# Two kinds of loads put behind small VectorE memsets, a longer pause ahead of the taps, and new shares for the convolution in a fused H3 and feed-forward kernel

## The chip, the cores and the metric

The kernel runs on one core of one Trainium2 chip. The metric is the device time of one execution in microseconds (us). The number given for a kernel is the median of several executions; the profile is of one execution, taken by the hardware profiler.

## The reference

For x of 2048 rows by 576 columns, the result is x plus two branches that both read the layer-normalised x. One is a feed forward with 4608 hidden columns; the other is an H3 block, a short convolution over four rows, a product with v, a convolution as long as the sequence, and a gate by the normalised x. In outline, with the shapes in comments:

```python
xn = _layernorm(x)                          # 2048 x 576
# feed forward
h = maximum(xn @ w1, 0)                     # 576 x 4608
ffn = h @ w2                                # 4608 x 576
# H3
k_shift = sum(k[rows - 3 + j] * shift_k[:, j] for j in range(4))
kv = k_shift * v
y = irfft(rfft(kv, 4096) * rfft(ssm_k, 4096))[:2048] + kv * ssm_D
return x + xn * y + ffn
```

## The kernel before

**Two strands on one TensorE.** The feed forward is the main strand. The 2048 rows are 16 tiles of 128 rows, in four blocks of four tiles (512 rows). Its hidden columns are 18 pairs of 256 columns, and `n` counts pairs: `n` = 0 to 17 for blocks 0 and 1, then `n` = 18 to 35 for blocks 2 and 3 (the second half; the change between them is the half turn). All products run in a 12 bit split: every operand is a rounded part and a rest, and three products of parts make one. In the first half the hidden values come from `mm1` (L513, psh), in the second from `quad` (L489, psa and psb), which needs seven block products in place of eight. `relu` makes the rounded hidden part hh on ScalarE (L495) and the rest ll on VectorE (L496). `unit` (L576, pso) multiplies with w2, and VectorE adds the result to the accumulator tiles acc (L580 and L584).

**Weights.** `load_w1(n)` brings one pair's first weights into the raw tile r1, of which there is one buffer: a 512 KB load (L395) and two small ones (L397). `load_w2` (L404) brings 288 KB into r2, two buffers. ScalarE rounds them (g at L413, w at L475), POOL (GpSimd) makes the rests (L384). In this text g1_0 is the first g made of pair 1's r, which the order prints as g_0 out of r_1, and r_1 that raw tile. A raw tile can be loaded again once POOL has read it for the last time.

**Normalised rows.** Blocks 0 and 1 are normalised and transposed at the start (`first_xT`, `second_xT`): statistics (L171, L172), `inv_std` (L178 to L183, with one square root on ScalarE, L179), the normalisation (L186) and the transposes on TensorE (L252 and L268). Blocks 2 and 3 are prepared during the first half by `later_xT`, piece by piece: it loads a block's rows into a scratch tile (L303, rows), takes their statistics, normalises, transposes, splits and stores the results to HBM as kept_b1, kept_b2, kept_t and kept_xr. `fetch` brings them back around the half turn.

**The convolution** is the other strand, a generator, `conv`. It has four stages. FK turns the filter: 12 loads of 384 KB bring it into the tile kr (L650), VectorE transposes pieces of it (L664, tr), `stack` splits them (L619 on ScalarE, L620 on VectorE, ks), and TensorE multiplies (L626). FX does the same with the input: the four taps (L725, L728, L729), the product with v (`gate`, L734), `stack` (xs), TensorE (L626, psf out of xs and wx), and the result zx goes to HBM. FM (L807) multiplies in the frequency domain, and FO (L958, L959) turns back what FM stored as zy; its loads are zo (L894), its splits ohi and olo (L914, L915).

**What sets the order.** After every few matmuls of the feed forward, `tick` is called with their cost in columns. It adds cost times a rate to the convolution's budget, and when the budget allows runs the next step of `conv`. A step yields a positive weight (W_FK, W_FX, W_FM, W_FO), which is taken from the budget, or a negative number, a pause: no step until so much of the feed forward has passed. START is the pause ahead of the first step. A step with `with here():` may be issued only behind the last accumulate and the last relu that the program has given out so far; a step without it has no such tie, and a scheduler lays it on its engine as early as its inputs and buffers let it. Nearly all loads go through one queue, SP, in the order in which they are issued, and each of SP's transfers waits for the one eight before it (its semaphore is one of DMAHW0 to DMAHW7).

**What the change touches.** The rows' loads in `later_xT` (L302 to L304), the filter's loads in `conv` (L646 to L652), the constants at L50, L55, L58 and L59, and the steps ahead of the loop over `T` in FX (L742 to L754).

Of the kernel before, what the change touches and what calls it, by code (L numbers as in the profile page):

```python
# [19 lines left out]
D = 576  # L20
# [3 lines left out]
NH = D // 2  # L24
# [7 lines left out]
BT = T // NB  # L32
# [14 lines left out]
W_STAGE = (12 * HR, 12 * HR, 12 * HR + 2 * 512, 6 * HR + 2 * 512)  # L47
W_UNIT = 12 * NH
PAUSE = 16000
START = 4000  # L50
SHARE = 0.96


N_FK, N_FX, N_FM, N_FO = 4 * T, 4 * T, 6 * NG, 4 * T
W_FK, W_FX, W_FM, W_FO = 1.75, 4.3, 1.62, 2.65  # L55
Q = 32
KB = 3
KT_GAP = 4500  # L58
PAUSES = 4 * NH // Q // KB * KT_GAP / PAUSE + 8  # L59
FFT_TOTAL = N_FK * W_FK + N_FX * W_FX + N_FM * W_FM + N_FO * W_FO  # L60
W_QUAD = sum(W_STAGE)
FFN_TOTAL = NPAIR * HB * (W_PLAIN + W_QUAD + 2 * 4 * W_UNIT)
# [47 lines left out]
def h3_ffn_kernel(ctx: ExitStack, tc, x, k, v, shift_k, ssm_k, ssm_D, w1, w2, fwd, inv, mid, out):  # L110
    nc = tc.nc
    x = x[0].rearrange("(p u t) d -> u p t d", u=U, t=T)
# [35 lines left out]
    def halves(u):  # L148

        return slice(u * A1, (u + 1) * A1), slice((1 - u) * A1, (2 - u) * A1)  # L150

    def move(tile_, rows, t, store=False, queues=(nc.sync, nc.sync)):
        for u in range(U):
            a, b = tile_[halves(u)[0]], rows[u, :, t]
            queues[u].dma_start(*((b, a) if store else (a, b)))
# [50 lines left out]
    def scratch(s, name):  # L206
        return xp.tile([P, N_FLOATS["t"]], F32, tag=f"t{s}", name=name, bufs=1)
# [77 lines left out]
    def later_xT(b):  # L285

        s = b % HB
        hold, area = scratch(0, f"rows{b}"), scratch(1, f"area{b}")
# [11 lines left out]
        r12 = slice(0, HR), slice(HR, 512)  # L300

        for i in range(0, BT, 2):  # L302
            move(hold[:, i * D:(i + 2) * D].rearrange("p (t d) -> p t d", t=2), x,  # L303
                 slice(b * BT + i, b * BT + i + 2))  # L304
        yield
        yield
        for i in range(BT):
# [303 lines left out]
    def load_const(pool, src, name):  # L611
        w = pool.tile([P, 2, P], F32R, tag="wt", name=name, bufs=3)
        nc.gpsimd.dma_start(w, src)
        return w

    def stack(dst, src, u):

        own, other = halves(u)
        nc.scalar.activation(dst[own], src[own], AF.Copy)  # L619
        nc.vector.tensor_tensor(dst[other], src[own], dst[own], OP.subtract)  # L620

    def first(w, stk, z, u):

        ps = fft_psum()
        for n in range(2):
            nc.tensor.matmul(ps[:, :NH], w[:, n, :], stk, start=n == 0, stop=n == 1)  # L626
        nc.scalar.activation(z, ps[:, :NH], AF.Copy)  # L627

    @contextmanager
    def here():  # L630


        with tc.issue_after(done["acc"].ins), tc.issue_after(done["act"].ins):
            yield

    def conv():
# [4 lines left out]
        with tc.tile_pool(name="fk", bufs=2) as fp:  # L641
            kr = fp.tile([P, NH // Q, 32 * A2], F32, tag="kr", name="kr", bufs=1)
            skip = fp.tile([P, NH], F32, tag="z", name="skip", bufs=3)
            for h in range(2):
                nc.sync.dma_start(skip[h * A1:h * A1 + 1, :], ssm_D[None, h * NH:(h + 1) * NH])
            for b in range(0, NH // Q, KB):  # L646
                for q in range(4):
                    h, r = divmod(q, 2)
                    src = ssm_k[h * NH + b * Q:h * NH + (b + KB) * Q, r * 32 * A2:(r + 1) * 32 * A2]
                    nc.sync.dma_start(kr[q * Q:(q + 1) * Q, b:b + KB, :],  # L650
                                      src.rearrange("(b d) l -> d b l", d=Q))
                    yield -KT_GAP  # L652
            ws = {}
            for n in range(3):
                ws[n] = load_const(fp, fwd[n // U][:, n % U], f"wk{n}")
            yield -PAUSE
            turned_ = {}

            def transpose(i):
                t2 = order[i]  # L660
                pool, tag = (xp, "m5") if i % 2 else (fp, "tr")
                tr = turned_[i] = pool.tile([P, NH], F32, tag=tag, name=f"tr{t2}", bufs=1)
                with here():
                    nc.vector.transpose(tr.rearrange("p (b q) -> p b q", q=Q),  # L664
                                        kr.rearrange("p b (q t) -> p b q t", t=A2)[:, :, :, t2])
                    if t2 == 0:
                        for h in range(2):
                            row = slice(h * A1, h * A1 + 1)
                            nc.vector.tensor_tensor(tr[row, :], tr[row, :], skip[row, :], OP.add)

            def prepare(i, h):
                if h == 0:
                    transpose(i)
                stk = fp.tile([P, NH], F32R, tag="stk", name=f"ks{order[i]}_{h}", bufs=3)
                with here():
                    stack(stk, turned_[i], h)
                return stk

            order = [T * u + t for t in range(T) for u in range(U)]
            nxt = []  # L680
            for h in range(2):
                nxt.append(prepare(0, h))
                yield -PAUSE / 8
            for n, t2 in enumerate(order):
                stk, nxt = nxt, []
                u, t = divmod(t2, T)
                for h in range(2):
                    z = fp.tile([P, NH], F32, tag="z", name=f"zk{t2}_{h}", bufs=3)
                    first(ws[n], stk[h], z, u)
                    nc.sync.dma_start(zk[:, t2, h * NH:(h + 1) * NH], z)  # L690
                    if n + 1 < len(order):
                        nxt.append(prepare(n + 1, h))
                    yield W_FK
                if n + 3 < len(order):
                    ws[n + 3] = load_const(fp, fwd[(n + 3) // U][:, (n + 3) % U], f"wk{n + 3}")


        with tc.tile_pool(name="fx", bufs=2) as fp:
# [32 lines left out]
            def gate(t):  # L731
                if t < T:
                    with here():
                        nc.vector.tensor_tensor(sums[t], sums[t], gates[t], OP.mult)  # L734

            def split(t, u):
                if t < T:
                    stks[t, u] = fp.tile([P, D], F32R, tag="stk", name=f"xs{t}_{u}", bufs=3)
                    with here():
                        stack(stks[t, u], sums[t], u)  # L740

            for t in range(1 - KS, 2):  # L742
                load(t)
            yield -PAUSE
            for n in range(KS):
                tap(0, n)
                yield -PAUSE / 8
            gate(0)
            for u in range(U):
                split(0, u)  # L750
            yield -PAUSE / 8
            for n in range(KS):
                tap(1, n)
                yield -PAUSE / 8  # L754
            for t in range(T):
                if t + 2 < T:
                    load(t + 2)
# [124 lines left out]
        with tc.tile_pool(name="fo", bufs=2) as fp:  # L882
# [62 lines left out]
            for n, (t, u) in enumerate(units):  # L945
                i = n // U
# [26 lines left out]


    stream = conv()
    clock = {"ffn": 0.0, "conv": 0.0, "until": START, "done": False}
    rate = FFT_TOTAL / (SHARE * FFN_TOTAL - PAUSES * PAUSE - START)

# [92 lines left out]
    for q, (n, s) in enumerate(visits):  # L1071
        half, m = divmod(n, NPAIR)
        b = half * HB + s
# [66 lines left out]
```

## Time and profile before

| | us |
|---|---|
| median of 3 executions | 1091.36 |
| lowest and highest of them | 1091.06, 1092.84 |
| the profiled execution, whole | 1092.71 |
| its span in the trace | 1090.9 |
| TensorE busy in it (7185 matmuls) | 1062.3 |

The span is what the trace shows from its first to its last instruction; 1.8 us of the execution lie outside it. Engines are PE (TensorE matmuls), PEld (TensorE weight loads), DVE (VectorE), ACT (ScalarE), POOL (GpSimd) and SP (SyncE, here a DMA queue, SPq). L384 is line 384 of the kernel. In a row of the timeline stand the start, the duration, engine, line, operation, output and inputs, the number of instructions drawn together, and in square brackets how long the engine stood idle before, and for whom. In a row of waits the three numbers are the idle time in all, how many times, and the longest. In a row of windows stand the stretch and its length, the busy time of PE, PEld, DVE, ACT and POOL, the TensorE clock that was granted (1.00 is full), the busy share of the DMA engines, and GB/s. A row of a tile or line gives the least, median and largest duration in ns, and the first and last start. A row of DMA issues ends with the median from issue to landing. A row of the chain gives start, duration and what ran.

### The profile page before, as it was taken

What the parts mean: (1) busy time and instruction counts of PE and PEld (TensorE: products, weight loads), DVE (VectorE), ACT (ScalarE), POOL (GpSimd) and SP (SyncE); (2) the same over time, 40 slices, a digit from 0 to 9 for tenths busy, and PEclk for the clock granted to TensorE, in tenths of its full rate; (3) what the DMA queues carried; (4) which work ended last, traced back from release to release, by engine and by line L of the source; (5) the groups of instructions that cost most, each with busy time, mean ns of one, the idle gap of its engine ahead of it and who ended that gap; (6) DMA issues with size and microseconds to landing.
All of it is one profiled execution on the core that took longest, in us unless ns stands there. A gap on an engine that the chain in (4) does not pass through costs nothing.

```text
span 1090.9 us, 19696 instructions
## 1 busy us (share of the span) xinstructions
PE 1062.3 (97%) x7185; PEld 997.7 (91%) x7185; DVE 769.8 (71%) x1277; ACT 560.6 (51%) x1221; POOL 394.7 (36%) x395
## 2 busy tenths in 40 slices
PE   7699999999999999999999999999999999999998
PEld 4589999998889999999999999999999999999998
DVE  5326777758999887743577767777767647878785
ACT  3123655643434433332686776678768645544451
POOL 3032323332323323223334433433434445445641
PEclk9899999999999999999999999999999999999999
DMA  9822565577566576334977545544555365545634
GB/s 222 187 72 67 154 191 167 152 231 210 153 202 199 157 227 183 116 89 133 302 226 216 162 140 153 143 145 132 147 149 151 109 170 143 159 121 159 194 118 109
DMA packets 117037, 176.12 MB, mean 161 GB/s; under 512 B 12269, under 2 KB 77551, under 8 KB 116172
## 3 DMA queue, kind: packets, MB, share of 16 engines
q1 hardware_dynamic: 104044, 160.68, 50.6%
q0 software_dynamic: 12576, 13.44, 5.2%
q8 instruction: 57, 0.93, 0.4%
q10 hardware_dynamic: 320, 0.74, 0.3%
q14 instruction: 40, 0.33, 0.1%
HBM read 122.12 MB, written 43.25 MB: 152 GB/s over the span
## 4 chain that ended last, share of the span: by engine, by line
PE 84%; DVE 6%; DMA 5%; ACT 2%; issue 1%; SPq 1%; DVEq 0%; ACTq 0%
PE pso L576 37%; PE psh L513 19%; PE psb L489 12%; PE psf L807 6%; PE psa L489 6%; PE psf L626 3%; DMA r<-in_w 2%; DVE c L729 1%; DVE e L728 1%; DMA kr<-in_ssm_k 1%; PE psf L958 1%; PE psf L268 1%; PE psf L959 1%; DMA ztx<-zx 1%; DMA rows<-in_x 1%
## 5 line engine op out<-in xcount | busy, mean ns | idle before, releaser
L576 PE MATMUL pso<-w,hh 128*128 128x288 f32 x2304 | 476.6, 296 | 2.2 <-DVE acc L580 1.3
L576 PEld LDWEIGHTS pso<-w,hh 128*128 128x128 f32 x2304 | 375.8, 188 | 10.4 <-ACT hh L495 2.0
L576 PE MATMUL pso<-w,ll 128*128 128x288 f32 x1152 | 331.6, 296 | 0.5 <-DVE ll L496 0.5
L384 POOL TENSOR_TENSOR g<-r,g 128x256 fp32r<-128x256 f32 (+2 forms) x145 | 165.3, 1146 | 441.1 <-ACT g L413 356.0
L513 PE MATMUL psh<-b,g 128*128 128x512 f32 x864 | 222.0, 398 | 0.3 <-ACT b L218 0.3
L576 PEld LDWEIGHTS pso<-w,ll 128*128 128x128 f32 x1152 | 214.2, 189 | 1.7 <-DVE ll L496 0.8
L513 PEld LDWEIGHTS psh<-b,g 128*128 128x128 f32 x864 | 158.4, 190 | 30.8 <-ACT b L218 0.9
L584 DVE TENSOR_TENSOR acc<-pso,acc 128x288 f32<-128x288 f32 x224 | 99.1, 451 | 69.6 <-PE pso L576 68.4
L384 POOL TENSOR_TENSOR w<-r,w 128x576 fp32r<-128x576 f32 x72 | 115.6, 1606 | 31.4 <-ACT w L475 31.2
L495 ACT ACTIVATE hh<-psh 128x512 fp32r<-128x512 f32 x72 | 43.0, 598 | 144.5 <-PE psh L513 144.4
L496 DVE SCALAR_TENSOR_TENSOR ll<-psh,hh 128x512 fp32r<-128x512 f32 x72 | 49.4, 686 | 71.4 <-ACT hh L495 70.9
L413 ACT ACTIVATE g<-r 128x256 fp32r<-128x256 f32 (+2 forms) x145 | 76.7, 542 | 38.8 <-DMA r<-in_w 36.6
L489 PE MATMUL psb<-t,g 128*128 128x256 f32 x648 | 94.5, 281 | 1.6 <-DVE psa L544 1.6
L489 PEld LDWEIGHTS psb<-t,g 128*128 128x128 f32 x648 | 85.1, 188 | 3.0 <-DVE psa L544 2.3
L442 POOL TENSOR_TENSOR r<-r 128x256 f32<-128x256 f32 x72 | 61.7, 876 | 41.4 <-DMA r<-in_w 39.8
L489 PE MATMUL psa<-b,g 128*128 128x256 f32 x432 | 62.7, 280 | 0.0
L489 PE MATMUL psb<-b,g 128*128 128x256 f32 x432 | 57.6, 280 | 0.0
L627 ACT ACTIVATE zx<-psf 128x288 f32<-128x288 f32 x64 | 25.4, 407 | 61.5 <-PE psf L626 48.9
L489 PEld LDWEIGHTS psa<-b,g 128*128 128x128 f32 x432 | 56.5, 188 | 0.0
L489 PEld LDWEIGHTS psb<-b,g 128*128 128x128 f32 x432 | 54.3, 188 | 0.1
L580 DVE SCALAR_TENSOR_TENSOR acc<-pso,rstd,acc 128x288 f32<-128x288 f32 x80 | 40.5, 509 | 17.3 <-PE pso L576 16.5
L475 ACT ACTIVATE w<-r 128x576 fp32r<-128x576 f32 x72 | 48.5, 675 | 0.1
(135 smaller groups left out, 1692.8 us busy)
## 6 DMA issues: line engine op xcount, KB each, us to landing
r<-in_w SPq DMA_DIRECT2D x72, 288.0 KB, 3.6
r<-in_w SPq DMA_DIRECT2D x35, 512.0 KB, 4.2
zk<-zk SPq DMA_DIRECT2D x64, 144.0 KB, 2.1
zx<-zx SPq DMA_DIRECT2D x32, 288.0 KB, 2.8
ztk<-zk SPq DMA_DIRECT2D x32, 288.0 KB, 3.9
ztx<-zx SPq DMA_DIRECT2D x32, 288.0 KB, 2.9
k<-k SPq DMA_DIRECT2D x64, 144.0 KB, 3.0
zy<-vo SPq DMA_DIRECT2D x32, 288.0 KB, 2.1
```

The costliest lines, as they stand in the source:

```text
L384: return nc.gpsimd.tensor_tensor(dst, src, hi, OP.subtract)
L413: nc.scalar.activation(hi, src, AF.Copy)
L442: nc.gpsimd.tensor_tensor(dst, a, b, op)
L475: nc.scalar.activation(t[:, 0], r2, AF.Copy)
L489: nc.tensor.matmul(ps, a, m, start=start and i == 0, stop=i == len(seq) - 1, skip_group_check=not start)
L495: done["act"] = nc.scalar.activation(hh, ps, AF.Relu)
L496: lows.append(nc.vector.scalar_tensor_tensor(ll, ps, 0.0, hh, op0=OP.max, op1=OP.subtract))
L513: nc.tensor.matmul(ps, a, m, start=i == 0, stop=i == len(seq) - 1)
L576: nc.tensor.matmul(ps[:, :NH], a, m, start=c == 0, stop=c == len(seq) - 1)
L580: done["acc"] = nc.vector.scalar_tensor_tensor(acc[t][:, dc], ps[:, :NH], rstd[:, t:t + 1], acc[t][:, dc], op0=OP.mult, op1=OP.add)
L584: done["acc"] = nc.vector.tensor_tensor(acc[t][:, dc], ps[:, :NH], acc[t][:, dc], OP.add)
L807: nc.tensor.matmul(ps[:, :NH], a, m[:, cols], start=n == 0, stop=n == 2)
```

## The change

Ahead of each pair of rows' loads in `later_xT` and ahead of each of the three groups of four filter loads, a VectorE memset clears one column of the tile that the load is going to fill, under `here()`. Since the load overwrites that column, it waits for the memset, and the memset stands in VectorE's queue behind the accumulate and the relu of its place. Further, START goes from 4000 to 12000 and the pause between filter loads from 4500 to 2000, the weights of three stages change, the pause ahead of the taps is doubled, and small pauses between the first splits and taps are added or lengthened. What is computed stays the same.

```diff
-START = 4000
+START = 12000
...
-W_FK, W_FX, W_FM, W_FO = 1.75, 4.3, 1.62, 2.65
+W_FK, W_FX, W_FM, W_FO = 1.25, 4.95, 1.5, 2.65
...
-KT_GAP = 4500
-PAUSES = 4 * NH // Q // KB * KT_GAP / PAUSE + 8
+KT_GAP = 2000
+PAUSES = 4 * NH // Q // KB * KT_GAP / PAUSE + 10
...
         for i in range(0, BT, 2):
-            move(hold[:, i * D:(i + 2) * D].rearrange("p (t d) -> p t d", t=2), x,
-                 slice(b * BT + i, b * BT + i + 2))
+            with here():
+                nc.vector.memset(hold[:, i * D:i * D + 1], 0.0)
+                move(hold[:, i * D:(i + 2) * D].rearrange("p (t d) -> p t d", t=2), x,
+                     slice(b * BT + i, b * BT + i + 2))
...
             for b in range(0, NH // Q, KB):
+                with here():
+                    nc.vector.memset(kr[:, b:b + KB, :1], 0.0)
                 for q in range(4):
...
             for t in range(1 - KS, 2):
                 load(t)
-            yield -PAUSE
+            yield -2 * PAUSE
             for n in range(KS):
                 tap(0, n)
                 yield -PAUSE / 8
             gate(0)
+            yield -PAUSE / 8
             for u in range(U):
                 split(0, u)
-            yield -PAUSE / 8
+                yield -PAUSE / 8
             for n in range(KS):
                 tap(1, n)
-                yield -PAUSE / 8
+                yield -PAUSE / 4
```

Three places of the order follow, of the kernel before and of the changed one; lines of the changed kernel are two to five higher. The first is SP near the program's start, with what each load waits for. Before, twelve rows from the eighth filter load on:

```order
L650 DMA kr<-in_ssm_k 32x3x1024 [waits DMAHW6_49]
L650 DMA kr<-in_ssm_k 32x3x1024 [waits DMAHW7_49]
L395 DMA r_1_227<-in_w 128x4x256 [waits DMASW2_49,DMASW1_49,DMAHW0_49,DMASW0_49,Pool_49]
L397 DMA r_1_227<-in_w 64x256 [waits DMAHW1_49]
L397 DMA r_1_227<-in_w 64x256 [waits DMAHW2_49]
L404 DMA r_1_0_234<-in_w 128x2x288 [waits DMAHW3_49,Pool_49]
L650 DMA kr<-in_ssm_k 32x3x1024 [waits DMAHW4_49]
L155 DMA rows_673<-in_x 64x1152 [waits DMAHW5_49,DVE_49,PE_49]
L404 DMA r_1_1_239<-in_w 128x2x288 [waits DMAHW6_49,Pool_49]
L155 DMA rows_673<-in_x 64x1152 [waits DMAHW7_49]
L155 DMA rows_673<-in_x 64x1152 [waits DMAHW0_49]
L155 DMA rows_673<-in_x 64x1152 [waits DMAHW1_49]
```

The changed kernel, from the row behind the two skip loads on:

```order
L397 DMA r_1_227<-in_w 128x4x256 [waits DMASW2_49,DMASW1_49,DMAHW7_49,DMASW0_49,Pool_49]
L399 DMA r_1_227<-in_w 64x256 [waits DMAHW0_49]
L399 DMA r_1_227<-in_w 64x256 [waits DMAHW1_49]
L406 DMA r_1_0_234<-in_w 128x2x288 [waits DMAHW2_49,Pool_49]
L406 DMA r_1_1_239<-in_w 128x2x288 [waits DMAHW3_49,Pool_49]
L654 DMA kr<-in_ssm_k 32x3x1024 [waits DMAHW4_49,DVE_49]
L654 DMA kr<-in_ssm_k 32x3x1024 [waits DMAHW5_49]
L654 DMA kr<-in_ssm_k 32x3x1024 [waits DMAHW6_49]
L654 DMA kr<-in_ssm_k 32x3x1024 [waits DMAHW7_49]
L654 DMA kr<-in_ssm_k 32x3x1024 [waits DMAHW0_49,DVE_49]
L654 DMA kr<-in_ssm_k 32x3x1024 [waits DMAHW1_49]
L654 DMA kr<-in_ssm_k 32x3x1024 [waits DMAHW2_49]
```

All of pair 1's weights moved ahead of all filter loads, and the first of each filter group now waits for VectorE. Behind these come one more filter load, r_2 with its small loads and r_2_0, then the last four filter loads around r_2_1; the rows of block 2 come behind r_3.

The second place is VectorE at the first input of FX. xs_0 and xs_1 of c are the parts of the first input, c its gated taps, rows is block 3's scratch tile. Before:

```order
L620 TENSOR_TENSOR xs_0_2560<-c_2442,xs_0_2560 64x576 [waits Activation_49]
L728 TENSOR_TENSOR e_2_2663<-k-1_2353,sk 128x576 [waits DVE_49]
L620 TENSOR_TENSOR xs_1_2563<-c_2442,xs_1_2563 64x576 [waits Activation_49]
L584 TENSOR_TENSOR acc_221<-pso_5_1_2912,acc_221 128x288 [waits PE_49]
L172 BN_AGGR mv<-bn_2904 128x2 [waits DVE_49]
L172 BN_AGGR mv<-bn_2908 128x2 [waits DVE_49]
```

Right ahead of these stood four statistics of block 3's rows (L171), of which the first waits for two of the rows' loads. The changed kernel, from the gate on:

```order
L738 TENSOR_TENSOR c_2339<-c_2339,v_2171 128x576 [waits DMAHW0_49,DVE_49]
L732 TENSOR_TENSOR e_1_2573<-k_2168,sk 128x576
L304 MEMSET rows_2746 128x1 [waits DMAHW1_49]
L304 MEMSET rows_2746 128x1
L498 SCALAR_TENSOR_TENSOR ll_0_1_2805<-psh_0_1_2779,hh_0_1_2804 128x512 [waits Activation_49]
L733 TENSOR_TENSOR c_2549<-c_2549,e_1_2573 128x576 [waits DVE_49]
L586 TENSOR_TENSOR acc_224<-pso_6_0_2808,acc_224 128x288 [waits PE_49]
L622 TENSOR_TENSOR xs_0_2485<-c_2339,xs_0_2485 64x576 [waits Activation_49]
L622 TENSOR_TENSOR xs_1_2510<-c_2339,xs_1_2510 64x576 [waits Activation_49]
```

The statistics moved behind both xs; the memsets stand ahead, and the first of them waits for the store of block 2's last rows (kept_xr), which used the same tile.

The third place is ScalarE around the same input. Before:

```order
L495 ACTIVATE hh_0_0_2869<-psh_0_0_2836 128x512
L413 ACTIVATE g_0_2896<-r_9_2808 128x512
L475 ACTIVATE w_8_0_2899<-r_8_0_2590 128x576
L619 ACTIVATE xs_0_2560<-c_2442 64x576
L619 ACTIVATE xs_1_2563<-c_2442 64x576
```

The changed kernel:

```order
L621 ACTIVATE xs_0_2485<-c_2339 64x576
L621 ACTIVATE xs_1_2510<-c_2339 64x576
L327 ACTIVATE area_679<-area_679 128x256
L497 ACTIVATE hh_0_0_2896<-psh_0_0_2870 128x512
L477 ACTIVATE w_8_0_2927<-r_8_0_2600 128x576
L629 ACTIVATE zx_0_2695<-psf 128x288 x2
L629 ACTIVATE zx_1_2764<-psf 128x288
L415 ACTIVATE g_0_2924<-r_9_2843 128x512
```

g9_0 (g_0 out of r_9) moved from ahead of the first xs to behind the first products' copies (zx); a piece of block 2's split (area) now stands in between.

## The prediction

> **What bounds the kernel now.** The page first: the share of each engine over the whole span.
>
> ```profile
> PE 1062.3 (97%) x7185; PEld 997.7 (91%) x7185; DVE 769.8 (71%) x1277; ACT 560.6 (51%) x1221; POOL 394.7 (36%) x395
> ```
>
> TensorE (PE) is busy for 97% of 1090.9 us. Only what the change takes from PE's idle time, or from PE time at a lowered clock, can count, since the matmuls stay the same 7185. So next comes the list of what PE waited for.
>
> ```profile
> PE psf L268 <- DVE xn L186: 9.6, 1, 9.6
> PE psf L626 <- issue: 2.6, 1, 2.6
> ...
> PE psf L807 <- ACT vo L863: 0.9, 1, 0.9
> ```
>
> One wait of 9.6 us stands out, L268, the transposes of block 1; the other large one this change can reach is L626, the conv's first product. The windows place both, with the clock (PEclk) that PE had there.
>
> ```profile
> 27.00:35.00 8.00, 4.26 (x30) 4.02 (x30) 2.46 (x8) 0.00 (x0) 0.00 (x0) 1.00 1.03 214
> 35.00:45.00 10.00, 3.47 (x14) 2.92 (x14) 5.05 (x13) 2.02 (x5) 1.26 (x1) 0.59 1.07 243
> 45.00:55.00 10.00, 9.77 (x45) 7.80 (x44) 3.79 (x7) 3.37 (x7) 0.95 (x1) 0.89 0.48 103
> ...
> 258.00:261.00 3.00, 0.72 (x6) 0.48 (x4) 2.12 (x5) 1.12 (x2) 1.41 (x2) 1.00 1.00 229
> 261.00:264.00 3.00, 2.67 (x13) 2.39 (x14) 2.91 (x8) 1.01 (x3) 0.56 (x1) 0.69 0.49 134
> 264.00:267.00 3.00, 3.00 (x13) 2.53 (x13) 3.00 (x8) 0.11 (x1) 0.00 (x0) 0.74 0.37 118
> 306.00:309.00 3.00, 1.74 (x13) 1.52 (x12) 2.94 (x6) 2.77 (x5) 0.00 (x0) 1.00 0.88 272
> 309.00:312.00 3.00, 2.76 (x14) 2.55 (x13) 2.97 (x6) 1.79 (x6) 1.24 (x2) 0.66 0.67 214
> 312.00:315.00 3.00, 3.00 (x13) 2.57 (x12) 3.00 (x7) 0.83 (x2) 0.00 (x0) 0.78 0.95 298
> ```
>
> From 27 to 45 us the DMA engines are full (share above 1) while PE, VectorE and ScalarE stand still. From 258 us PE idles 2.28 + 0.33 and from 306 us 1.26 + 0.24 us, 4.1 us in all, and after each gap the clock falls: 3 x (0.31 + 0.26 + 0.34 + 0.22) = 3.4 us more. So the X stage holds 7.5 us of loss.
>
> **Part 1, the filter's loads (kr) go behind the next weights.** The chain of work and the timeline show what ends the long wait.
>
> ```profile
> 14.63 8.53 DMA kr<-in_ssm_k
> 23.25 14.63 DMA r<-in_w
> ```
>
> ```profile
> 17.32 0.46 POOL L384 TENSOR_TENSOR g<-r,g 128x128 fp32r<-128x128 f32 x1 [0.34 <-ACT g L413]
> 21.95 1.08 ACT L495 ACTIVATE hh<-psh 128x512 fp32r<-128x512 f32 x2 [0.98 <-PE psh L513]
> ...
> 28.91 0.16 DVE L178 TENSOR_SCALAR q<-mv 128x4 f32<-128x4 f32 x1
> ...
> 37.90 0.63 ACT L413 ACTIVATE g<-r 128x512 fp32r<-128x512 f32 x1 [14.86 <-DMA r<-in_w]
> 38.43 0.19 ACT L179 ACTIVATE q<-q 128x4 f32<-128x4 f32 x1
> ...
> 40.63 2.05 DVE L186 TENSOR_SCALAR xn<-acc,mv,rstd 128x576 f32<-128x576 f32 x4
> ...
> 41.27 2.82 PE L268 MATMUL psf<-ident,xn 128*128 128x128 f32 x12 [9.63 <-DVE xn L186]
> ```
>
> ScalarE's queue holds g1_0 (L413, reads r_1) ahead of the square root (L179) that the normalisation needs. r_1 is issued at 23.25, behind nine kr loads, shares the engines with them, and lands at 37.88. ScalarE stands for 14.86 us, though VectorE had the root's input ready at 28.91 + 0.16 = 29.07. In the changed order r_1 stands ahead of all kr; it then waits only for its buffer's last reader, the POOL row, which ends at 17.32 + 0.46 = 17.78.
>
> ```profile
> kr<-in_ssm_k SPq DMA_DIRECT2D x12, 384.0 KB, 10.7
> ```
>
> ```profile
> r<-in_w SPq DMA_DIRECT2D x35, 512.0 KB, 4.2
> ```
>
> At 4.2 us r_1 lands at about 22.1. g1_0 now runs between the two hh of 21.95 and puts the second back by its 0.63 us, ahead of VectorE's need. The root runs at 29.1. From root to first transpose took 41.27 - 38.43 = 2.84 us, so PE starts at about 32.0 instead of 41.27. PE's last matmul before it ended 9.63 earlier, at 31.64, and the two memsets near there cost by their nearest row
>
> ```profile
> 1.09 0.06 DVE L1011 MEMSET table<- 128x1 f32 x1
> ```
>
> 0.06 us each. The gap falls from 9.63 to 0.4 to 0.9 us: I take **-9.0**. Second, the clock. By the granted 0.59 and 0.89 PE lost 3.73 x 0.41 = 1.5 us from 41.27 to 45 and 10 x 0.11 = 1.1 to 55; part of it lies beside waits for ScalarE's copies, so I take about half of the 2.6, **-1.4**, with 0 and -2.6 as ends. If r_1 is late, g1_0 holds the second hh instead: from 23.5 on each microsecond costs one. Its latest plausible landing is by the kr row, 17.8 + 10.7 = 28.5, and 5 us are then lost again. Part 1 is -10.4, between -5 and -12.
>
> [...] In the rows above a gap of 2.6 us, and one of 1.3 us, were each followed by a stretch with 0.66 to 0.78 granted. [...]
>
> What is queued behind the held loads needs three more rows of VectorE's and SP's timelines and of the tile kr.
>
> ```profile
> 56.07 0.39 SPq L395 DMA_DIRECT2D r<-in_w  x1
> ```
>
> ```profile
> 68.91 0.46 DVE L584 TENSOR_TENSOR acc<-pso,acc 128x288 f32<-128x288 f32 x1 [1.60 <-PE pso L576]
> ```
>
> ```profile
> L664 DVE STREAM_TRANSPOSE tr<-kr x32: 645/707/727, 93.3 to 219.3; 128x288 f32<-128x288 f32 x32
> ```
>
> SP issues in order, so r_2 stands behind kr 1 to 8, whose second group waits for a memset among the root's steps, at about 31 us. 8 x 384 KB at the 214 to 243 GB/s of the windows take 13 to 15 us, to about 45. r_2 came at 56.07, when r_1 had been read, and that is 45.7 with 10.4 us less ahead of it: the two just meet, and I cost this at nothing; if they don't, a late r_2 costs what it is late. The third group waits for a memset right behind the accumulate of 68.91, so at about 58.5 + 0.5 = 59, and lands at 70 by the 10.7 us row. The first transpose of kr stood at 93.3; its place in the order is 6.5 us of matmul time earlier (the first filter product moves from 78.0 to 71.5) and 10.4 us are gone, so it comes at 76. **Cover 6 us**, no cost.
>
> **Part 2, rows 3, the longer pause and the taps.** Before the X stage the order is this.
>
> ```profile
> 254.09 0.76 DVE L734 TENSOR_TENSOR c<-c,v 128x576 f32<-128x576 f32 x1
> ...
> 256.03 0.64 ACT L413 ACTIVATE g<-r 128x512 fp32r<-128x512 f32 x1 [5.14 <-DMA r<-in_w]
> ...
> 257.15 1.38 ACT L619 ACTIVATE xs<-c 64x576 fp32r<-64x576 f32 x2
> ...
> 258.85 1.54 DVE L171 BATCH_NORM_STATS2 bn<-rows 128x6 f32<-128x288 f32 x4 [1.70 <-DMA rows<-in_x]
> ...
> 260.42 0.75 DVE L620 TENSOR_TENSOR xs<-c,xs 64x576 fp32r<-64x576 f32 x1
> ...
> 261.27 0.76 PE L626 MATMUL psf<-xs,wx 128*128 128x288 f32 x4 [2.55 <-issue]
> ```
>
> The gated input was done at 254.09 + 0.76 = 254.85, but ScalarE's xs stood behind g9_0, which waited for its weights (5.14), and VectorE's xs behind statistics that waited for rows 3. In the changed order neither stands ahead: ScalarE's xs follows the gate at once, the statistics come after both xs. By the rows, 0.7 + 0.75 after the gate xs is ready, 4.9 us earlier against the gate, for a wait of 2.55. What is added on VectorE: a memset that waits for the store of the earlier rows (in the order 17 rows of VectorE behind what it stores), and a few pieces of the earlier rows' splitting that were over before. Later lag comes from VectorE being full.
>
> ```profile
> 250.00:300.00 50.00, 47.37 (x277) 42.46 (x276) 47.76 (x81) 20.13 (x40) 15.38 (x15) 0.97 0.63 174
> 300.00:350.00 50.00, 48.51 (x287) 43.88 (x286) 48.64 (x77) 21.37 (x43) 16.12 (x16) 0.97 0.63 189
> ```
>
> The share of 4.95 for 4.3 spreads the X products over 15% more conv budget; in the order the 32 inputs stretch from 232 to 259 us of matmul time, 11%. A step's ten operations of 0.75 us (the tap rows below) take 7.5 of 14.5 us before and of 16.2 after: VectorE goes from 96% to about 91%. I leave 2.1 of the 7.5 us lost: **-5.4**, from -7.5 (all gone) to 0 (VectorE or the weights' wait takes its place).
>
> [...]
>
> ```profile
> L728 DVE TENSOR_TENSOR e<-k,sk x42: 741/750/1737, 254.8 to 467.7; 128x576 f32<-128x576 f32 x42
> ```
>
> A tap takes 0.75 us, at worst 1.74. [...]
>
> **Part 3, the rest.** The first product of the FM stage moves from 486 to 503 us of matmul time, just behind the half turn, where kept operands are fetched; the one FM wait now is 0.9 us. I add **0.8** (0 to 4). Ahead of FO the order leaves 11.8 us instead of 20.0 between the last FM and the first FO product.
>
> ```profile
> L894 SPq DMA_DIRECT2D zo<-zy x32: 319/326/1329, 884.0 to 1051.1; - x32
> L914 ACT ACTIVATE ohi<-zo x32: 669/675/681, 897.9 to 1063.4; 128x576 fp32r<-128x576 f32 x32
> ...
> DMA to landing us min/median/max: 2.8/3.1/5.5
> ```
>
> The first load landed by 884.0 + 3.1 = 887.1 and was split at 897.9, 10.8 us in hand; 8.2 go, 2.6 are left: no cost (up to 3 with the 5.5). START and KT_GAP move when conv steps come, not how many.
>
> Sum against the profiled execution (span 1090.9, 1.8 outside, 1092.71 in all): -10.4 - 5.4 + 0.8 = -15.0, so 1077.7. The median is 1.35 lower than that execution: **1076.4**.
>
> **Rivals.**
> A. Start alone: the taps stay late, by collisions with POOL (1 us each, the 1.74 row) or by xs 1 behind g9_0, whose load now follows rows 3 and a store. For it: VectorE at 96%. Against: xs 0 loses both known waits. 1076.4 + 5.4 = 1081.8.
> B. The turn or FO: a product waits for a fetch or zo. With 4 instead of 0.8, 1079.6; with both, 1082.6.
> C. All gone: -12 - 7.5 + 0, 1071.9.
> D. The change doesn't do what it says: r_1, though ahead of kr, is still late because accumulator loads fill the engines, landing at 28.5. Against: those loads are small, 288 KB each beside nine of 384. 5.4 of the 10.4 are lost: 1081.8.
> E. Slower. The third kr group becomes the bound: the transposes of kr stand in VectorE's queue ahead of the feed forward's own relu parts, so a late group stops everything. It decides once the group lands after 76, and from there a microsecond costs one: at 80 the time is 1080.4, and past 93.3, 34 us after issue where the row of full traffic has 10.7, it is slower than before by what can be told. Little speaks for it.
>
> **How the numbers follow.** Forecast (1073.5 to 1079.5) 0.52; A 0.22; B 0.10; C 0.08; D 0.03; E past the old time, 1094, 0.03; nothing gained 0.02. From 1071 to 1085 about 9 in 10 is held with the bounds of A, B and C; of the ends, start at -5 with X at 0 gives 1087 and is left out. 0.2%, 2.2 us, is about what can be told from no change: faster 0.95, same 0.02, slower 0.03.
>
> **What would show it.** Right: ScalarE's g1_0 near 22.5, its root near 29.1, the wait at L268 under 1.5 us, no lowered clock between 32 and 45; the first xs product with a wait under 1 us. Wrong: g1_0 waiting for r_1 past 24; a wait named kr; VectorE over 95% and lowered clocks in the 120 us after the first xs product; new waits at the first FM or FO product.

## The result

Four executions of the changed kernel took 1082.46 us in the median (1080.63 to 1083.12), four of the kernel before beside them 1092.10. The ratio is 0.9906, with a 95% interval of 0.9885 to 0.9927: faster by 0.9%. In a second comparison it was 0.9889 (0.9869 to 0.9909). The profiled execution took 1082.66 us; its page begins

```profile
span 1080.9 us, 19682 instructions
## 1 busy us (share of the span) xinstructions
PE 1060.0 (98%) x7185; PEld 995.2 (92%) x7185; DVE 764.7 (71%) x1284; ACT 558.2 (52%) x1221; POOL 394.4 (36%) x395
```

and its longest waits of PE are these; the one at L268 comes twelfth, with 0.3 us where it had 9.6. Lines stand two to five higher than in the kernel before.

```profile
PE pso L578 <- DVE acc L586: 2.3, 2, 1.6
PE psf L628 <- issue: 2.3, 2, 1.2
PE psb L491 <- DVE psb L549: 2.1, 3, 1.4
PE psb L491 <- DVE psa L546: 1.8, 3, 1.0
...
PE psf L268 <- DVE xn L186: 0.3, 1, 0.3
```

**The start.** The timeline of the changed kernel from 17 to 33 us, to be held against the rows of before:

```profile
17.38 0.39 SPq L397 DMA_DIRECT2D r<-in_w  x1
...
21.56 0.62 ACT L415 ACTIVATE g<-r 128x512 fp32r<-128x512 f32 x1
...
25.92 6.80 SPq L654 DMA_DIRECT2D kr<-in_ssm_k  x8
...
28.23 0.20 ACT L179 ACTIVATE q<-q 128x4 f32<-128x4 f32 x1 [5.56 <-DVE q L178]
...
32.58 2.02 PE L268 MATMUL psf<-ident,xn 128*128 128x128 f32 x12 [0.31 <-DVE xn L186]
```

r_1 leaves at 17.38 instead of 23.25 and has been read from 21.56 on; ScalarE now waits for the root's input, not for a load; the filter's loads follow at 25.92.

**The X stage.** The timeline from 231 to 246 us:

```profile
231.08 0.76 DVE L732 TENSOR_TENSOR e<-k-1_2164,sk 128x576 f32<-128x576 f32 x1 [6.18 <-DMA k-1_2164<-in_k]
...
236.71 0.53 PE L578 MATMUL pso<-w,hh 128*128 128x288 f32 x2 [1.60 <-DVE acc L586]
...
240.16 0.75 DVE L738 TENSOR_TENSOR c<-c,v 128x576 f32<-128x576 f32 x1
240.83 0.75 DVE L732 TENSOR_TENSOR e<-k,sk 128x576 f32<-128x576 f32 x1
241.51 0.68 DVE L498 SCALAR_TENSOR_TENSOR ll<-psh,hh 128x512 fp32r<-128x512 f32 x1
...
242.78 0.45 DVE L586 TENSOR_TENSOR acc<-pso,acc 128x288 f32<-128x288 f32 x1
243.26 2.68 DVE L622 TENSOR_TENSOR xs<-c,xs 64x576 fp32r<-64x576 f32 x2
...
243.91 1.41 POOL L386 TENSOR_TENSOR w<-r,w 128x576 fp32r<-128x576 f32 x1 [3.96 <-ACT w L477]
...
244.11 0.77 PE L628 MATMUL psf<-xs,wx 128*128 128x288 f32 x4 [1.10 <-issue]
...
246.04 0.82 PE L628 MATMUL psf<-xs,wx 128*128 128x288 f32 x2 [1.15 <-issue]
```

VectorE stands 6.18 us for the first input's load, an accumulate behind the taps is late for PE (1.60), and PE then waits twice for xs. The stage lost its old waits and has new ones of about the same sum.

To compare many kernels one sum serves better than lists of waits, since it takes in short gaps and the lowered clock. For each matmul the distance from its start to the next one's start is taken, less the usual distance for its shape (0.133 us for 288 columns, 0.232 for 512, 0.117 for 256, 0.109 for 128), and the rests are added up by stretch. The text calls this PE's loss. The usual distances of all matmuls ahead of a product, added up, are its place in matmul time: where PE would reach it without any loss. Over the whole span the loss is 39.5 us before and 29.7 after; the difference of 9.8 is that of the two profiled executions, 1092.71 - 1082.66 = 10.05, but for 0.25. By stretch:

| kernel | median us | ratio to before (95%) | 0 to 60 | 220 to 340 | from 540 | all |
|---|---|---|---|---|---|---|
| before | 1092.10 | 1 | 23.3 | 8.6 | 7.6 | 39.5 |
| changed | 1082.46 | 0.9906 (0.9885 to 0.9927) | 12.9 | 8.3 | 8.4 | 29.7 |
| changed, again (e9) | 1080.36 | 0.9889 (0.9869 to 0.9909) | 11.8 | 7.0 | 8.6 | 27.5 |
| e1 filter's memsets alone | 1079.84 | 0.9891 (0.9874 to 0.9908) | 11.2 | 7.9 | 6.7 | 25.9 |
| e3 changed, without them | 1093.26 | 1.0015 (1.0002 to 1.0028) | 24.2 | 7.7 | 10.2 | 42.2 |
| e4 changed, no rows' memsets | 1081.78 | 0.9908 (0.9892 to 0.9925) | 12.4 | 7.6 | 8.9 | 28.9 |
| e5 changed, pause of 6 | 1079.62 | 0.9888 (0.9874 to 0.9903) | 13.5 | 5.2 | 8.9 | 27.6 |
| e6 changed, POOL reads out | 1079.39 | 0.9874 (0.9857 to 0.9890) | 12.5 | 4.3 | 9.8 | 26.7 |
| e7 filter's memsets, pause of 6 | 1072.55 | 0.9809 (0.9793 to 0.9825) | 11.8 | 1.7 | 3.9 | 19.1 |
| e8 changed, old weights | 1087.88 | 0.9958 (0.9939 to 0.9978) | 13.3 | 13.4 | 8.3 | 34.9 |
| e10 changed, old START, KT_GAP, W_FK | 1090.92 | 0.9977 (0.9955 to 0.9999) | 11.4 | 7.6 | 20.2 | 39.1 |
| e11 e7, with rows' memsets, new weights | 1081.07 | 0.9897 (0.9870 to 0.9923) | 11.8 | 4.2 | 12.2 | 28.3 |
| e12 pause of 6 alone | 1084.08 | 0.9917 (0.9888 to 0.9946) | 22.8 | 3.4 | 5.2 | 31.5 |
| e13 changed, pause of 1 | 1081.23 | 0.9895 (0.9869 to 0.9921) | 12.5 | 8.9 | 7.2 | 28.7 |

The ratios are to runs of the kernel before on the same chip, whose medians were 1091.45 (e1, e3, e4, e5), 1092.81 (e6 to e9) and 1093.72 (e10 to e13); between these groups compare ratios, not medians.

### The profile page after: what moved, and what is told of

Same layout as the page of the kernel before. It is cut to its first block, busy times and chain, and to the rows that moved or that the text cites. A ratio compares the mean times of both kernels' runs of the same rounds, so it can differ in the third digit from the quotient of the medians.

```text
span 1080.9 us, 19682 instructions
## 1 busy us (share of the span) xinstructions
PE 1060.0 (98%) x7185; PEld 995.2 (92%) x7185; DVE 764.7 (71%) x1284; ACT 558.2 (52%) x1221; POOL 394.4 (36%) x395
## 4 chain that ended last, share of the span: by engine, by line
PE 86%; DVE 6%; DMA 3%; ACT 2%; issue 2%; SPq 0%; POOL 0%; DVEq 0%; POOLq 0%; ACTq 0%
PE pso L578 38%; PE psh L515 18%; PE psb L491 13%; PE psf L812 7%; PE psa L491 5%; PE psf L628 3%; DMA r<-in_w 2%; DMA sk<-in_shift_k 1%; DVE c L733 1%; PE psf L268 1%; DVE xs L622 1%; DVE e L732 1%; DMA k<-in_k 1%; PE psf L964 1%; DVE y L966 1%
## 5 line engine op out<-in xcount | busy, mean ns | idle before, releaser
L578 PE MATMUL pso<-w,hh 128*128 128x288 f32 x2304 | 475.5, 296 | 4.1 <-DVE acc L586 2.3
L578 PEld LDWEIGHTS pso<-w,hh 128*128 128x128 f32 x2304 | 376.1, 189 | 12.6 <-DVE acc L586 2.8
L578 PE MATMUL pso<-w,ll 128*128 128x288 f32 x1152 | 330.7, 296 | 0.5 <-DVE ll L498 0.5
L386 POOL TENSOR_TENSOR g<-r,g 128x256 fp32r<-128x256 f32 (+2 forms) x145 | 165.9, 1150 | 430.5 <-ACT g L415 402.8
L515 PE MATMUL psh<-b,g 128*128 128x512 f32 x864 | 218.4, 395 | 0.9 <-ACT b L218 0.7
L578 PEld LDWEIGHTS pso<-w,ll 128*128 128x128 f32 x1152 | 214.4, 189 | 1.7 <-DVE ll L498 0.8
L586 DVE TENSOR_TENSOR acc<-pso,acc 128x288 f32<-128x288 f32 x224 | 99.3, 451 | 67.2 <-PE pso L578 65.9
L386 POOL TENSOR_TENSOR w<-r,w 128x576 fp32r<-128x576 f32 x72 | 112.6, 1565 | 49.6 <-ACT w L477 49.4
L582 DVE SCALAR_TENSOR_TENSOR acc<-pso,rstd,acc 128x288 f32<-128x288 f32 x80 | 40.7, 512 | 21.4 <-PE pso L578 20.7
```

Of the source, the lines that this page charges most:

```text
L386: return nc.gpsimd.tensor_tensor(dst, src, hi, OP.subtract)
L515: nc.tensor.matmul(ps, a, m, start=i == 0, stop=i == len(seq) - 1)
L578: nc.tensor.matmul(ps[:, :NH], a, m, start=c == 0, stop=c == len(seq) - 1)
L582: done["acc"] = nc.vector.scalar_tensor_tensor(acc[t][:, dc], ps[:, :NH], rstd[:, t:t + 1], acc[t][:, dc], op0=OP.mult, op1=OP.add)
L586: done["acc"] = nc.vector.tensor_tensor(acc[t][:, dc], ps[:, :NH], acc[t][:, dc], OP.add)
```

## The experiments

**e1, the filter's memsets alone.** The kernel before with two lines:

```diff
             for b in range(0, NH // Q, KB):
+                with here():
+                    nc.vector.memset(kr[:, b:b + KB, :1], 0.0)
                 for q in range(4):
```

> The kernel before with the memsets ahead of the filter's loads alone. Theory S (the gain is the start: r_1 no longer behind nine filter loads): the wait at L268 falls from 9.6 to under 3 us (in this order the four loads of block 2's rows, 4 x 288 KB or some 5 us at 230 GB/s, have slipped ahead of r_1, so r_1 lands some 5 us later than in the changed kernel, where it was read at 21.6), and the time is 1082 to 1088. Theory L (the gain comes from the later conv steps: START, KT_GAP and the shares): the wait at L268 may shrink, but the time stays within 3 us of before, 1089 to 1094.

1079.84 us, ratio 0.9891: the two added lines give as much as the whole change. Theory S holds, and the time is 2 us below its range. That block 2's rows, now ahead of r_1, would make it land some 5 us later was right, but it cost nothing; the timeline of e1:

```profile
26.10 0.63 ACT L413 ACTIVATE g<-r 128x512 fp32r<-128x512 f32 x1 [4.19 <-DMA r<-in_w]
...
28.15 0.20 ACT L179 ACTIVATE q<-q 128x4 f32<-128x4 f32 x1 [1.42 <-DVE q L178]
...
30.81 2.02 PE L268 MATMUL psf<-ident,xn 128*128 128x128 f32 x12 [0.30 <-DVE xn L186]
```

g1_0 comes 4.5 us later than in the changed kernel, but still ends at 26.73, ahead of the root's input at 28.1. In this order it stands behind both hh, so it holds nothing up. r_1 has some 6 us of room in this order; nine filter loads were more than that, four rows loads are not.

**e3, the changed kernel without those lines.**

> The changed kernel without the memsets ahead of the filter's loads; rows' memsets, START, KT_GAP, shares and pauses stay. Theory S: nine filter loads stand ahead of r_1 again, the wait at L268 is back at 9 to 10 us and the time at 1090 to 1094. Theory L: START at 12000 keeps most of the gain, 1082 to 1086.

1093.26, and L268 waits again:

```profile
PE psf L268 <- DVE xn L186: 10.9, 1, 10.9
```

START, KT_GAP, weights, pauses and the rows' memsets together, without the filter's memsets, are worth nothing (ratio 1.0015, slower if anything). START at 12000 doesn't move the filter's loads: in e3 nine of them are issued ahead of r_1 (from 13.42 us, r_1 at 23.36).

**e4, the changed kernel without the rows' memsets** and without the `here()` around them and the loads.

```diff
         for i in range(0, BT, 2):
-            with here():
-                nc.vector.memset(hold[:, i * D:i * D + 1], 0.0)
-                move(hold[:, i * D:(i + 2) * D].rearrange("p (t d) -> p t d", t=2), x,
-                     slice(b * BT + i, b * BT + i + 2))
+            move(hold[:, i * D:(i + 2) * D].rearrange("p (t d) -> p t d", t=2), x,
+                 slice(b * BT + i, b * BT + i + 2))
```

> The changed kernel without the rows' memsets. In its order block 2's four rows loads (288 KB each) stand ahead of r_1 at the start, and block 3's are free to go early. If the place of any large load ahead of r_1 counts: r_1 is read at 25 to 28 instead of 21.6, the wait at L268 or the waits just ahead of it grow by 2 to 5 us, and the time is 1084 to 1088. If only the filter's loads count (they are 384 KB and nine): 1081 to 1084.

1081.78, no different from the changed kernel. Four rows loads ahead of r_1 cost nothing, as in e1: of the first expectation the late r_1 came (it is read at 26.73), the loss didn't.

**e13 and e5, the pause ahead of the taps.** In the changed kernel, 1 and 6 in place of 2 (PAUSES lowered by 1 and raised by 4):

```diff
-            yield -2 * PAUSE
+            yield -6 * PAUSE
```

> The changed kernel with the pause ahead of the taps as before (once instead of twice). The first xs product stands at 227.0 us of matmul time in place of 227.3, so if the pause of 2 is swallowed by the filter stage's lag, the time is within 1.5 us of the changed kernel (1080 to 1084) and the loss between 220 and 340 within 1.5 of 7 to 8.3; if the doubling counted, the loss there grows by 2 us or more.

> The changed kernel with the pause ahead of the taps at 6 times instead of 2 times (and the sum of pauses raised by 4). Theory P (the pause of 2 is used up by the lag of the filter stage: its last product runs far behind its place in the program, so the taps go as soon as their loads land and the first input's products come too early for VectorE): the taps start at the same row of VectorE's order, the first xs product comes some 15 us of matmul time later, the waits for xs and for acc near 235 to 245 (1.8, 1.3 and 1.3 us, with the lowered clock behind them) shrink to under 1 us together, and the time falls by 3 to 6 us to 1076 to 1080. Theory D (VectorE is full through the whole stage): the waits move later but stay, 1081 to 1084.

With 1 the time is 1081.23 and the loss of the X stage 8.9: the doubling did nothing that can be told. With 6 the loss falls from 8.3 to 5.2, and the first xs product has no wait of note. The time, ratio 0.9888, is at the upper end of theory P and not clear of the changed kernel's; of 5.2 us the greater part is one later wait of 2.3 us, at an xs product (L628), and the lowered clock (0.97 granted from 238 to 302, where e6 below has 1.00: by that some 1.9 us). Ahead of the xs of 278.89 stands a collision, in the timeline of VectorE and then of POOL:

```profile
270.73 1.42 DVE L729 TENSOR_TENSOR c<-k,sk 128x576 f32<-128x576 f32 x1
272.07 1.98 DVE L733 TENSOR_TENSOR c<-c,e 128x576 f32<-128x576 f32 x1
```

```profile
270.02 1.51 POOL L386 TENSOR_TENSOR g<-r,g 128x512 fp32r<-128x512 f32 x1
271.50 1.95 POOL L386 TENSOR_TENSOR w<-r,w 128x576 fp32r<-128x576 f32 x1
```

Each of the two VectorE operations, which take 0.75 us elsewhere, ends 0.6 us after the POOL operation it met (272.15 after 271.53, 274.05 after 273.45), as if it had started only then.

**e6, POOL without its reads.** The changed kernel; for pairs 8 to 11 the rests of the weights are zeros, so what the products with them add is left out.

```diff
-    def split_lo(dst, src, hi):
+    def split_lo(dst, src, hi, out=False):
+        if out:
+            return nc.gpsimd.memset(f32(dst), 0.0)
         return nc.gpsimd.tensor_tensor(dst, src, hi, OP.subtract)
...
-        split_lo(lo, src, hi)
+        split_lo(lo, src, hi, 8 <= n <= 11)
...
-        last = split_lo(t[:, 1], r2, t[:, 0])
+        last = split_lo(t[:, 1], r2, t[:, 0], 8 <= n <= 11)
```

> The changed kernel in which POOL, for pairs 8 to 11 alone, fills the rests of the weights with zeros instead of reading the raw weights and subtracting (that part of the product is left out). POOL then reads no SBUF there; the order stays. Theory C (collisions: a VectorE operation with two SBUF inputs stands still while POOL reads): the two xs operations of 2.68 us at the first input take 0.75 each, no tap between 240 and 300 takes over 0.9, the second wait at the first xs (1.3 us) falls under 0.4, and PE's loss between 220 and 340 falls from 8.3 by 2 to 5 us; time 1077 to 1080.5. Theory L (only the late loads and the backlog behind them count): the operations keep durations over 1.2 us or the waits stay within 1 us of 8.3 in all, 1081 to 1083.5.

Between 238 and 302 us the changed kernel starts 54 taps, gates and xs, of which eight take over 0.9 us (1.25 to 1.90); e6 starts 55, and none takes over 0.9 (0.76 at most, or 1.54 for two xs). The windows of that stretch, of the changed kernel and then of e6:

```profile
238.00:302.00 64.00, 60.60 (x353) 54.25 (x352) 63.27 (x106) 25.43 (x53) 20.38 (x20) 0.97 0.65 187
```

```profile
238.00:302.00 64.00, 62.00 (x369) 55.28 (x368) 60.56 (x114) 28.49 (x59) 10.39 (x20) 1.00 0.73 206
```

VectorE does eight operations more in 2.7 us less. The two xs of the first input, in the timeline of e6:

```profile
241.51 1.54 DVE L624 TENSOR_TENSOR xs<-c,xs 64x576 fp32r<-64x576 f32 x2
```

The pair takes 1.54 us instead of 2.68, the second wait at the first xs is gone, and the stage's loss falls from 8.3 (7.0 in the second profile) to 4.3. Theory C holds for the operations and for the stage: 2.7 to 4.0 us of its loss go with POOL's reads. The time itself, 1079.39, isn't clear of the 1080.36 of the changed kernel on the same chip (e9, below). Since POOL's memsets are also shorter (0.5 us for 1.3 to 1.9), the run doesn't part a shorter POOL operation from one that doesn't read; the coincidences in e5 and the missing slow taps speak for the second. The changed kernel's whole trace shows the meetings: of its 128 taps and gates, which have two inputs in SBUF, 101 met no subtraction of POOL's (L386) and took 0.76 us at most; 27 met one, and 17 of these took 1.14 to 2.88, each ending 0.61 to 0.63 us after a subtraction had ended. Of its 224 accumulates at L586, which have one input in PSUM, 97 met a subtraction, and none took over 0.46, nor did the others. The two xs of the first input agree: 2.68 us for two operations that met one POOL operation, 1.54 without.

Of the 4.3 us left, one wait shows the second half of rival A. ScalarE's parts of the second input stand behind g9_0, which waits for its weights, and VectorE's parts and PE wait in turn, in the timelines of ScalarE and VectorE and the waits of PE:

```profile
253.53 0.63 ACT L417 ACTIVATE g<-r 128x512 fp32r<-128x512 f32 x1 [9.42 <-DMA r<-in_w]
```

```profile
255.05 1.54 DVE L624 TENSOR_TENSOR xs<-c,xs 64x576 fp32r<-64x576 f32 x2 [1.78 <-ACT xs L623]
```

```profile
PE psf L630 <- DVE xs L624: 1.5, 1, 1.5
```

The second input's gate had ended at 251.8. The changed kernel's second profile has the same wait, with 1.1 us; its first has none there.

**e8, the changed kernel with the stage weights of before.**

```diff
-W_FK, W_FX, W_FM, W_FO = 1.25, 4.95, 1.5, 2.65
+W_FK, W_FX, W_FM, W_FO = 1.75, 4.3, 1.62, 2.65
```

> The changed kernel with the stage weights of before (1.75, 4.3, 1.62). If the new weights help VectorE keep up (13 us longer X stage): the loss between 220 and 340 grows by 1 us or more, 1083 to 1086. If they do nothing there and cost later (new waits of psb on VectorE after 540): the loss after 540 falls from 8.5 to about 7 and the time to 1080 to 1082.

1087.88, above both ranges: the new weights are worth 5.7 to 7.5 us to the rest of the change (by the ratios to its two measurements). The stage's loss grows from 8.3 to 13.4, more than expected, and the loss after 540 stays. VectorE's wait for the first input's load, 6.18 us in the changed kernel, is longer here, and the accumulates behind it cost PE more, as its timeline and then its waits show:

```profile
235.41 0.83 DVE L732 TENSOR_TENSOR e<-k-1_2290,sk 128x576 f32<-128x576 f32 x1 [10.68 <-DMA k-1_2290<-in_k]
```

```profile
PE pso L578 <- DVE acc L586: 5.9, 3, 3.5
PE psf L628 <- DVE xs L622: 4.0, 3, 3.1
```

Why its load lands later still was not tried.

**e10, the changed kernel with START, KT_GAP and W_FK of before.**

```diff
-START = 12000
+START = 4000
-W_FK, W_FX, W_FM, W_FO = 1.25, 4.95, 1.5, 2.65
+W_FK, W_FX, W_FM, W_FO = 1.75, 4.95, 1.5, 2.65
-KT_GAP = 2000
+KT_GAP = 4500
```

> The changed kernel with START, KT_GAP and W_FK of before: the filter stage stands where it stood (78 to 207 us of matmul time instead of 72 to 199), the first xs product at 234 instead of 227; the memsets, the doubled pause and the other new weights stay. Theory E (moving the filter stage earlier put block 2's last splits on VectorE into the first input's taps, and that cost the X stage): the loss between 220 and 340, 7 to 8.3 in the changed kernel, falls to 3 to 5.5, time 1076 to 1080. Theory F (the distance from the filter's last product to the first xs product counts, and that is 28 us in both): the loss stays at 7 to 8.5, time 1080 to 1083.

The loss of the X stage stays at 7.6, so theory F is the nearer one there. But the time is 1090.92, which neither theory gave: from 540 us on the loss is 20.2. The X stage's products now end at 503 us of matmul time and FM begins at 521, behind the half turn; VectorE stands 6.99 us for a split whose load (ztk) is late, and an accumulate behind it makes PE wait, as VectorE's timeline and then PE's waits show:

```profile
558.72 0.76 DVE L803 TENSOR_TENSOR lok<-ztk,hik 128x576 fp32r<-128x576 f32 x1 [6.99 <-ACT hik L802]
559.40 0.45 DVE L586 TENSOR_TENSOR acc<-pso,acc 128x288 f32<-128x288 f32 x1
```

```profile
PE pso L578 <- DVE acc L586: 6.6, 3, 3.8
```

The changed kernel thus needs the new START, KT_GAP and W_FK beside its other edits. Why is not shown. Of the 11.8 us that e10 loses more from 540 us on, some 5.3 lie between 540 and 640 and some 4.5 between 910 and 1000, in FO. And the later place of FM alone isn't the cause: in e5 FM begins at 520 and in e11 (below) at 532, and from 540 to 580, where e10 loses 5.6, they lose 0.3 and nothing.

**e9, the changed kernel again**, beside e6 to e8.

> The changed kernel itself, beside the others on one chip: 1081 to 1083.5 by every theory. It tells whether the memsets alone (1079.84) were really faster than the whole change (1082.46).

1080.36, just below the range, ratio 0.9889 with a loss of 7.0 in the X stage. So the memsets alone (0.9891) are not faster than the whole change. The sum of the stage differs that much between two executions of one kernel (8.3 and 7.0), and differences of 1 to 2 us in it tell nothing.

**e7, e12 and e11: memsets and pause apart and together.** e7 is e1 with a pause of 6 times ahead of the taps (before: once, PAUSES raised by 5), e12 that pause without the memsets, e11 is e7 with the rows' memsets and with 4.95 and 1.5 for W_FX and W_FM.

> The kernel before with two edits only: the memsets ahead of the filter's loads, and a pause ahead of the taps of 6 times instead of once (the sum of pauses raised by 5). First xs product 13 us of matmul time later than before. Theory P (the start's gain and the X stage's are independent, and xs comes too early for VectorE): the start stays as with the memsets alone, the loss between 220 and 340 falls from 7.9 to 3 to 5 us, time 1073 to 1078. Theory D (what is late is VectorE's total load, so a later start of the stage only moves the waits): within 1.5 us of the memsets alone, 1078 to 1081.

> The kernel before with the 6 times pause alone. If start and X stage are independent, its gain adds to that of the memsets (11.6 alone, 20.3 with both): 7 to 10 us, 1083 to 1086, with L268 still waiting 9 to 11. If the pause pays only behind the early start: within 3 us of before.

> The memsets alone with the 6 times pause (1072.55) and, added, the rows' memsets and the new weights of two stages (4.95, 1.5). Theory G (more room still helps VectorE): the loss between 220 and 340 falls from 1.7 to under 1 and the time to 1070 to 1072.5. Theory H (the X stage now ends past the half turn and later stages are squeezed): the loss after 540, 3.9, grows by 2 to 5 us, 1073.5 to 1078.

e7 takes 1072.55 us, ratio 0.9809 (0.9793 to 0.9825): it beats both kernels. The windows from 220 to 340 us, of the kernel before and of e7:

```profile
220.00:340.00 120.00, 115.88 (x677) 104.33 (x676) 103.34 (x169) 46.30 (x96) 36.17 (x35) 0.97 0.67 194
```

```profile
220.00:340.00 120.00, 119.12 (x717) 107.65 (x716) 99.19 (x163) 43.28 (x88) 36.59 (x35) 1.00 0.64 185
```

PE is busy 3.2 us longer there and keeps its full clock. e12 alone gives 0.9917, e1 alone 0.9891, and their product 0.9809 is the ratio of e7: within the intervals the two gains add up, and theory P holds. Both sizes were better than it said: a loss of 1.7 for the 3 to 5 expected, and a time just below 1073 to 1078. In e12 L268 still waits 8.9 us (9 to 11 expected). e11 is slower, as theory H had it, but by more than its range: the loss after 540 grew by 8.3 us in place of 2 to 5, and the X stage's from 1.7 to 4.2. e11 doesn't part the rows' memsets from the two weights.

## Why the prediction was right, and where it was wrong

The range, 1071 to 1085, held the time; the predicted 1076.4 was 6.1 below it, and the forecast's own band, 1073.5 to 1079.5, missed it. The time came out at rival A's 1081.8: the start as forecast and nothing gained in the X stage. It came out there in part by luck, since one of the things that kept the X stage from gaining, a gate that came later, is in no rival.

**Start, -10.4.** Right, with its steps. r_1 was issued at 17.38 (forecast 17.8), g1_0 ran at 21.56 (22.5 in the list of what would show it), the root at 28.23 (29.1), the first transpose at 32.58 (32.0), with a wait of 0.31 (0.4 to 0.9). The loss of the first 60 us fell by 10.4, and by 11.5 in the second profile. e1 and e3 show that the place of the filter's loads is the cause. r_2 was issued at 45.72 (45.7). The cover of the held loads held: the first transpose of kr came at 76.2 (76), and nothing waited for kr.

```profile
L668 DVE STREAM_TRANSPOSE tr<-kr x32: 652/710/736, 76.2 to 202.1; 128x288 f32<-128x288 f32 x32
```

**X stage, -5.4.** Wrong: -0.3 by the loss, -1.6 in the second profile. The step that failed is that xs would be ready 4.9 us earlier against the gate, "for a wait of 2.55". Against the gate it was earlier, by 3.1 us: before, VectorE's first xs ended 6.3 us after the gate (254.85 to 261.17), and now PE takes it 3.2 us after (240.91 to 244.11). The forecast "0.7 + 0.75 after the gate" left out what its own order shows between gate and xs on VectorE, e, ll, c and acc: they kept it to 243.23. And the gate itself came 4.2 us later against the filter's last product, which the prediction took as unmoved, while the first xs product stands 28 us of matmul time behind that product in both kernels. Those products, before and after, the last start at the row's end:

```profile
L626 PE MATMUL psf<-ks,wk x128: 288/295/302, 102.1 to 230.7; 128*128 128x288 f32 x128
```

```profile
L628 PE MATMUL psf<-ks,wk x128: 288/295/302, 85.3 to 212.6; 128*128 128x288 f32 x128
```

The first tap that waited for the input, before:

```profile
246.95 0.76 DVE L728 TENSOR_TENSOR e<-k-1_2353,sk 128x576 f32<-128x576 f32 x1 [5.89 <-DMA k-1_2353<-in_k]
```

The gate ended 254.85 - 230.7 = 24.15 us after it before, and 240.91 - 212.6 = 28.31 after. Of the 4.2 us, 2.2 are the input's load, which VectorE had at 246.95 before (16.3 us after the last product) and at 231.08 now (18.5); the other 1.9 are the first taps, accumulates and pieces of block 2's splits between it and the gate. So the order did what it showed, and the slack went to the loads and to VectorE's work ahead of the gate. The loads of this stage are issued only behind the filter's last product, in both kernels, SP's first row before and after:

```profile
234.13 1.76 SPq L701 DMA_DIRECT2D sk<-in_shift_k  x4
```

```profile
216.78 2.01 SPq L705 DMA_DIRECT2D sk<-in_shift_k  x4
```

The doubled pause moved nothing: with 1, 2 and 6 times the pause the first xs product stands at 227, 227 and 240 us of matmul time. VectorE, forecast to fall from 96% to 91% busy, stood at 63.27 of 64 us from 238 to 302 (the windows of e6), which the prediction had named as a sign of being wrong. Both halves of rival A were met as well: e6 puts the collisions at 2.7 to 4.0 us of the loss, and xs of the second input behind g9_0 cost 1.1 us in the second profile and 1.5 in e6. Part of what is left is the clock: 0.50 was granted from 246 to 249 us in the first profile, and in the second it stayed full through the stage (1.00 from 220 to 340).

**Half turn and FO, +0.8.** The loss from 540 on rose from 7.6 to 8.4 (8.6), so the size was right, but by chance, for it was not at the places named. FO's first product had no wait to speak of and FM's first none; new are waits of the second half's `quad` for VectorE (2.1 at L549). The price of rival B, unmet in the changed kernel, has its like in e10 (a wait of 3.8 us behind the half turn), though e11, with FM still later, has no such wait.

**What the change is, then.** Its filter's memsets carry the gain. The weights, START and KT_GAP belong together: with the old weights the kernel loses 5.7 to 7.5 us (e8), with the other two and the filter stage's weight as they were 8 to 10 (e10), and all of them with the rows' memsets and pauses don't come out faster than the two lines alone (0.9906 and 0.9889 beside 0.9891).

## What to carry to other kernels

A load that nothing ties to its place goes as early as its buffer allows, and may stand in the queue ahead of one that everybody waits for (here nine filter loads ahead of r_1, and a wait of 9.6 us); a memset of one column at the right place holds it back, for 0.06 us of VectorE. Before moving work to a better place, look at what sets its time: here the taps were set by loads that were issued only behind the filter stage's last product, so an order that looked better, and a pause that was doubled, gave nothing, and only a pause of 6 times did. Edits that pay singly are worth trying without the edits beside them: the best kernel here has two of the seven parts, one of them at another size.

## What the runs showed of the hardware

The same gaps did not always bring the same clock. The changed kernel had the same gaps of PE in both profiles (0.5 us and then 1.4 us, the longest near it, at L578 for acc of L582), 0.4 us apart in their place. From 27 to 31 us one execution ran at 0.57 of the clock, and the other at full, as the windows of the first and the second profile show:

```profile
27.00:31.00 4.00, 4.00 (x21) 4.00 (x20) 2.41 (x11) 0.20 (x1) 0.00 (x0) 0.57 0.94 212
```

```profile
27.00:31.00 4.00, 4.00 (x30) 3.93 (x30) 3.60 (x15) 0.21 (x1) 0.00 (x0) 1.00 0.90 205
```

The first executed 21 matmuls there and the second 30. No gap in the 10 us ahead was longer than 1.4 us in either, so the length of the gaps doesn't tell the two apart; what does is not shown. From 32 to 45 us the clock stayed full in both profiles (1.00), as forecast. The wait at L268 fell by 9.3 us, and of the 10.4 and 11.5 us that the first 60 us gained this leaves 1.1 and 2.2 for the clock and all else, around the predicted 1.4.
